# A one-token attention and MLP kernel whose large loads move from SyncE's queue to GpSimd's

## The chip, the cores and the metric

The kernel runs on one core of a Trainium2 chip. The metric is the device time of that core in microseconds (us); lower is better. A profiled execution has a time of its own, and a span, which runs from its first to its last recorded instruction. Engine names are those of the profile: PE is TensorE's matrix multiply, PEld its weight load, DVE is VectorE, ACT is ScalarE, POOL is GpSimd, SP is SyncE. A "q" behind a name (SPq) is that engine's instruction queue, which also issues transfers.

## The reference

One token x of 512 values goes through two branches that a scalar gate mixes.

```python
x = A_x                                             # [1, 1, 512], bf16
g = sigmoid((x * gate_w).sum(-1))                   # one scalar
# attention branch: 32 heads of 128, 4096 cached keys and values a head
q = (x @ wq).reshape(32, 128)                       # wq [512, 4096]
scores = einsum("hd,hkd->hk", q, k_cache) * 128 ** -0.5   # k_cache [32, 4096, 128]
o = einsum("hk,hkd->hd", softmax(scores), v_cache)  # v_cache [32, 4096, 128]
a = o.reshape(4096) @ wo                            # wo [4096, 512]
# MLP branch: 512 -> 1376 -> 512
h = x @ w1 + b1
b = (relu(h) ** 2) @ w2 + b2
out = g * a + (1 - g) * b                           # [1, 1, 512]
```

Nearly all of the data is read once: 32 MiB of keys, 32 MiB of values, 4 MiB each of wq and wo, and 2.7 MiB of MLP weights, 78.3 MB in all. With one token there is little arithmetic for each byte.

## The kernel before

The program is written out by hand for each engine, with semaphores between them. No scheduler or tile pool changes its order.

**Loads.** A head's keys or values make one transfer of 1 MiB: 128 partitions, each with one contiguous row of 8,192 bytes (32 cached positions by 128 values). `Kt` and `Vt` have 8 slots each (`NK`, `NV`). SP issues all large loads, in this order. First come four 1 MiB slices of wq into the tile `W` (L200). Then come the keys of heads 0 to 6 (`LAG` = 7; L206). Then, for each head h, the values of h (L211) and the keys of h+7 (L206). Behind h = 8 go four slices of w1 (L221, 344 KB each), and behind h = 10 the two parts of w2 (L223, L224). When the last use of wq is over (`s_qps` at 8), five pieces of wo follow into the same tile `W` (L227). Last, SP waits for the result and issues the store (L230). From the ninth on, a key load first waits until its slot has been read by DVE (`s_sd`) and by PE (`s_t`), and a value load until PE has read its slot (`s_pv`). SP meets these waits in program order, so whatever is listed behind a waiting load waits too:

```python
def load_k(h):
    if h >= NK:
        eng.wait_ge(s_sd, h - NK + 1)
        eng.wait_ge(s_t, 2 * (h - NK + 1))
    eng.dma_start(Kt[:, h % NK, :], k_h[h, :, :]).then_inc(s_k[h % NK], 16)
```

**Small loads.** ACT issues x, the gate weights and the biases, 1 to 2.5 KB each.

**Constants.** POOL does no transfers. It fills `ident`, `identf`, `onesf`, `negs` and `sel` with memsets (L236 to L240) and turns three of them into patterns (L243, L246). Two semaphores report this: `s_cst` (`onesf` and `negs`) and `s_id`.

**Start of PE.** PE's first matmul (L304) sums the gate's products over partitions with `onesf`. It waits for `s_cst` and for DVE's product (`s_zp`). Its result goes to ACT for an exp (L263, `s_ez`). PE waits for all four slices of wq and for `s_ez` before it makes q (L310), then makes the first rows of q for DVE (`q_rows`, L320), and then waits for all of `s_id`.

**A head.** Half of its scores are made by DVE: 16 multiply-and-sum instructions over 128x128 blocks of `Kt` (`ttr`, L484). The other half goes over PE: 16 transposes (L334), ACT's copy of them (L275) and 16 matmuls (L344). Every four heads the maximum is found and ACT takes the exp. `pv` (L371) multiplies with the values seven steps behind the keys.

**End.** The MLP is put in at steps 24 and 30 (L387, L399). Behind the last head PE regroups the heads and multiplies with wo piece by piece as it lands (`attn_out`, L417). DVE adds (L552), PE transposes, DVE copies (L554), and SP stores.

## Time and profile before

| | |
|---|---|
| median of 3 runs | 202.94 us (202.88 to 203.29) |
| the profiled execution's own time | 203.75 us |
| its span | 202.0 us |
| busy: PE, PEld | 128.6, 115.2 us (64%, 57%) |
| busy: DVE, ACT, POOL | 127.7, 79.4, 2.4 us (63%, 39%, 1%) |
| read from HBM | 78.32 MB, 388 GB/s over the span |
| granted TensorE clock, mean | 0.614 of full speed |

The profile shows the busy time of each engine and of the 16 DMA engines, the chain of work that ended last, the groups of instructions, and what ended each idle stretch. A DMA issue is an instruction of a queue (SPq, ACTq), and is not counted as an engine's busy time; its duration is that of the issue and not of the transfer. "To landing" is from the issue to the last byte. A DMA packet here is one contiguous piece that one of the 16 DMA engines moves.

### The profile page before, as it was taken

How to read it: one execution, taken by the hardware profiler on the slowest of the kernel's cores; microseconds unless marked ns; L12 is line 12 of the kernel's file. 1: busy time of each engine (PE TensorE's matmuls, PEld its weight loads, DVE VectorE, ACT ScalarE, POOL GpSimd, SP SyncE). 2: the span in 40 equal slices, each digit the busy share in tenths (PEclk: the TensorE clock that was granted, in tenths of full speed). 3: DMA queues.
4: the chain of work that ended last, by engine and by line, in shares of the span. 5: the costliest groups of instructions: out<-in, count | busy, mean ns of one | idle time of the engine just before them, and what ended most of it. 6: DMA issues, size and time to landing. Idle time of an engine off the chain costs nothing.

```text
span 202.0 us, 6578 instructions
## 1 busy us (share of the span) xinstructions
PE 128.6 (64%) x2465; PEld 115.2 (57%) x2465; DVE 127.7 (63%) x1134; ACT 79.4 (39%) x147; POOL 2.4 (1%) x12
## 2 busy tenths in 40 slices
PE   0119924956998867528345694569876759864544
PEld 0017824755797667526345674568876759764443
DVE  0200999999999887626645778577877777710000
ACT  2000864566475436305324453435363336320000
POOL 4000000000000000000000000000000000000000
PEclk9999985675555555556655588557555555555555
DMA  5999999999999999999999999999999999999810
GB/s 205 385 395 428 420 420 415 422 417 422 420 419 415 419 413 415 420 426 373 417 425 415 419 417 420 419 422 420 417 417 417 423 417 422 417 419 420 329 66 8
DMA packets 11935, 78.74 MB, mean 390 GB/s; under 512 B 1824, under 2 KB 1920, under 8 KB 2688
## 3 DMA queue, kind: packets, MB, share of 16 engines
q1 hardware_dynamic: 11352, 78.32, 94.1%
q8 instruction: 19, 0.31, 0.6%
q10 hardware_dynamic: 552, 0.01, 0.1%
q14 instruction: 12, 0.10, 0.1%
HBM read 78.32 MB, written 0.00 MB: 388 GB/s over the span
## 4 chain that ended last, share of the span: by engine, by line
DMA 73%; DVE 13%; PE 7%; SPq 4%; issue 1%; ACT 0%; DVEq 0%
DMA Kt<-in_A_k_cache_dram 54%; DMA W<-in_A_wo_dram 13%; DVE Kt L484 12%; DMA W<-in_A_wq_dram 6%; PE KP L334 2%; PE pX L310 2%; PE pQ L320 1%; SPq L223 1%; SPq L206 1%; SPq L227 1%; DVE S L484 1%; SPq L200 1%; SPq L211 1%; PE pX L417 1%; PE pM L358 1%
## 5 line engine op out<-in xcount | busy, mean ns | idle before, releaser
L484 DVE CUSTOM_DVE_ANT_0 Kt<-Kt,qb 128x128 bf16<-128x128 bf16 x512 | 111.3, 286 | 28.5 <-DMA Kt<-in_A_k_cache_dram 28.1
L275 ACT ACTIVATE kT<-KP 128x1024 bf16<-128x1024 bf16 x64 | 61.8, 1021 | 69.3 <-PE KP L334 69.3
L334 PE MATMUL KP<-ident,Kt 128*128 128x128 bf16 x512 | 55.1, 294 | 36.1 <-DMA Kt<-in_A_k_cache_dram 36.0
L334 PEld LDWEIGHTS KP<-ident,Kt 128*128 128x128 bf16 x512 | 47.8, 136 | 38.5 <-DMA Kt<-in_A_k_cache_dram 37.5
L484 DVE DVE_READ_ACCUMULATOR2_ANT S<- 128x1 f32 x512 | 41.6, 81 | 0.0
L344 PE MATMUL pS<-qcol,kT 128*128 128x1 bf16 x512 | 19.3, 167 | 10.6 <-DVE S L490 10.3
L344 PEld LDWEIGHTS pS<-qcol,kT 128*128 128x128 bf16 x512 | 18.8, 107 | 12.2 <-DVE S L490 11.9
L371 PEld LDWEIGHTS pO<-E,Vt 128*128 128x128 bf16 x512 | 15.7, 104 | 1.7 <-issue 1.1
L371 PE MATMUL pO<-E,Vt 128*128 128x1 bf16 x512 | 16.2, 166 | 0.0
L320 PE MATMUL pQ<-W,xb 128*128 128x512 bf16 x32 | 13.8, 581 | 0.0
L267 ACT ACTIVATE qb<-pQ 128x512 bf16<-128x512 f32 x8 | 4.8, 597 | 20.4 <-PE pQ L320 20.3
L371 PE MATMUL pQ<-E,Vt 128*128 128x1 bf16 x256 | 8.0, 165 | 6.0 <-DMA Vt<-in_A_v_cache_dram 6.0
L371 PEld LDWEIGHTS pQ<-E,Vt 128*128 128x128 bf16 x256 | 7.6, 104 | 6.3 <-issue 6.3
L286 ACT ACTIVATE E<-S,nM 128x32 bf16<-128x32 f32 x32 | 9.9, 310 | 0.3
L310 PE MATMUL pX<-xcol,W 128*128 128x1 bf16 x128 | 3.6, 165 | 7.6 <-DMA W<-in_A_wq_dram 7.6
L371 PEld LDWEIGHTS pX<-E,Vt 128*128 128x128 bf16 x256 | 7.6, 101 | 1.0 <-issue 0.8
L310 PEld LDWEIGHTS pX<-xcol,W 128*128 128x128 bf16 x128 | 3.5, 104 | 7.7 <-issue 7.7
L371 PE MATMUL pX<-E,Vt 128*128 128x1 bf16 x256 | 7.8, 164 | 0.0
L472 DVE CAST qcol<-pX 128x32 bf16<-128x32 f32 x1 | 0.2, 192 | 10.4 <-PE pX L310 10.4
L493 DVE TENSOR_REDUCE mp<-S 128x1 f32<-128x32 f32 x32 | 6.0, 186 | 1.1
L417 PE MATMUL pX<-o,W 128*128 128x1 bf16 x128 | 4.1, 166 | 3.8 <-DMA W<-in_A_wo_dram 3.5
L490 DVE COPY S<-pS 128x16 f32<-128x16 f32 x32 | 5.4, 169 | 1.6 <-PE pS L344 1.6
(65 smaller groups left out, 55.2 us busy)
## 6 DMA issues: line engine op xcount, KB each, us to landing
Kt<-in_A_k_cache_dram SPq DMA_DIRECT2D x32, 1024.0 KB, 27.1
Vt<-in_A_v_cache_dram SPq DMA_DIRECT2D x32, 1024.0 KB, 27.3
W<-in_A_wq_dram SPq DMA_DIRECT2D x4, 1024.0 KB, 8.7
W<-in_A_wo_dram SPq DMA_DIRECT2D x3, 1024.0 KB, 22.6
w_sb<-in_B_w_dram SPq DMA_DIRECT2D x4, 344.0 KB, 22.0
w2a<-in_B_w_dram SPq DMA_DIRECT2D x1, 1280.0 KB, 18.1
W<-in_A_wo_dram SPq DMA_DIRECT2D x1, 768.0 KB, 25.6
W<-in_A_wo_dram SPq DMA_DIRECT2D x1, 256.0 KB, 24.1
```

The source lines that it names most:

```text
L267: eng.activation(qb[:, c * 512:(c + 1) * 512], pQ[:, :], ACT.Copy).then_inc(s_qb, 1)
L275: eng.activation(kT[:, h % 2, j * HB * 128:(j + 1) * HB * 128], KP[n % 3][:, :], ACT.Copy).then_inc(s_ev, 1)
L286: eng.activation(E[:, h % NE, :], S[:, h % NS, :], ACT.Exp, bias=nM[:, h:h + 1], scale=SCALE, accum_out=RS[:, h:h + 1]).then_inc(s_e, 1)
L310: mm = eng.matmul(Q[:, h:h + 1], wq_sb[:, t, h * 128:(h + 1) * 128], xcol[:, t:t + 1], start=(t == 0), stop=(t == 3))
L320: mm = eng.matmul(pQ[:, :], xb[:, t, :], wq_sb[:, t, c * 512:(c + 1) * 512], start=(t == 0), stop=(t == 3))
L334: mm = eng.transpose(KP[n % 3][:, y * 128:(y + 1) * 128], Kt[:, h % NK, b * 128:(b + 1) * 128], ident[:, :])
L344: mm = eng.matmul(S2[:, y:y + 1], kT[:, h % 2, y * 128:(y + 1) * 128], qcol[:, h:h + 1], start=True, stop=True)
L371: mm = eng.matmul(O(h, h + 1), Vt[:, h % NV, b * 128:(b + 1) * 128], E[:, h % NE, b:b + 1], start=(b == 0), stop=(b == NB - 1))
L417: mm = eng.matmul(acc[:, j:j + 1], wo_sb[:, t, j * 128:(j + 1) * 128], o2[:, t:t + 1], start=False, stop=(t == 31), skip_group_check=True)
L484: ins = eng.tensor_tensor_reduce(kb, kb, qb[:, h * 128:(h + 1) * 128], 1.0, 0.0, ALU.mult, ALU.add, S[:, h % NS, b:b + 1])
L490: eng.tensor_copy(S[:, h % NS, XB:NB], S2).then_inc(s_cp, 1)
L493: eng.tensor_reduce(mp[:, h:h + 1], S[:, h % NS, :], AX.X, ALU.max).then_inc(s_mp, 1)
```

## The change

The issue of all large loads moves from SP's program to POOL's, in the same order and with the same waits. SP keeps only the store of the result. POOL first issues the four slices of wq and the keys of heads 0 to 6, then makes its constants, and then goes on with the loads. The load of w1 is one transfer of 128 rows of 11,008 bytes instead of four of 128 rows of 2,752 bytes, so PE waits for 16 instead of 64 on `s_w1`. The two parts of w2 report on a semaphore each.

```diff
@@ semaphores
-        s_w2 = sem("s_w2")
+        s_w2 = [sem(f"s_w2{n}") for n in range(2)]
@@ block.sync
         def _(eng):
+            eng.wait_ge(s_f4, 1)
+            eng.dma_start(out[0, 0, :].rearrange("(j p) -> j p", p=128), fin4[:, :]).then_inc(s_out, 16)
+            eng.wait_ge(s_out, 16)
+
+        @block.gpsimd
+        def _(eng):
             for t in range(4):
                 eng.dma_start(wq_sb[:, t, :], wq_v[:, t, :]).then_inc(s_wq[t], 16)
...
             for h in range(LAG):
                 load_k(h)
-            for h in range(NH):
-                load_v(h)
-                if h + LAG < NH:
-                    load_k(h + LAG)
-                if h == 8:
-                    for t in range(4):
-                        eng.dma_start(w1_sb[:, t, :], w1_v[:, t, :]).then_inc(s_w1, 16)
-                if h == 10:
-                    eng.dma_start(w2a[:, :, :], w2_v).then_inc(s_w2, 16)
-                    eng.dma_start(w2b[:, :], B_w2[FG * 128:F, :]).then_inc(s_w2, 16)
-            eng.wait_ge(s_qps, 8)
-            for c in range(NW):
-                eng.dma_start(wo_sb[:, TS[c]:TS[c + 1], :], wo_v[:, TS[c]:TS[c + 1], :])\
-                   .then_inc(s_wo[c], 16)
-            eng.wait_ge(s_f4, 1)
-            eng.dma_start(out[0, 0, :].rearrange("(j p) -> j p", p=128), fin4[:, :]).then_inc(s_out, 16)
-            eng.wait_ge(s_out, 16)
-
-        @block.gpsimd
-        def _(eng):
             eng.memset(ident[:, :], 0.0).then_inc(s_id, 1)
...
             eng.affine_select(out=sel[:, :, :], in_=sel[:, :, :], compare_op=ALU.not_equal, fill=1.0,
                               base=0, pattern=[[1, 4], [-1, 128]], channel_multiplier=4)\
                .then_inc(s_id, 1)
+            for h in range(NH):
+                load_v(h)
+                if h + LAG < NH:
+                    load_k(h + LAG)
+                if h == 8:
+                    eng.dma_start(w1_sb[:, :, :], w1_v).then_inc(s_w1, 16)
+                if h == 10:
+                    eng.dma_start(w2a[:, :, :], w2_v).then_inc(s_w2[0], 16)
+                    eng.dma_start(w2b[:, :], B_w2[FG * 128:F, :]).then_inc(s_w2[1], 16)
+            eng.wait_ge(s_qps, 8)
+            for c in range(NW):
+                eng.dma_start(wo_sb[:, TS[c]:TS[c + 1], :], wo_v[:, TS[c]:TS[c + 1], :])\
+                   .then_inc(s_wo[c], 16)
@@ block.tensor
             def mlp_h():
-                eng.wait_ge(s_w1, 64)
+                eng.wait_ge(s_w1, 16)
...
             def mlp_out():
                 eng.wait_ge(s_hs, 2)
-                eng.wait_ge(s_w2, 32)
+                eng.wait_ge(s_w2[0], 16)
+                eng.wait_ge(s_w2[1], 16)
```

PE, DVE and ACT run the same instructions in the same order as before.

## The prediction

> **What bounds the kernel now.** I read the strip of 40 slices first. It asks whether the transfers ever stop, and from the second slice to the 37th they don't.

> ```profile
> DMA  5999999999999999999999999999999999999810
> GB/s 205 385 395 428 420 420 415 422 417 422 420 419 415 419 413 415 420 426 373 417 425 415 419 417 420 419 422 420 417 417 417 423 417 422 417 419 420 329 66 8
> q1 hardware_dynamic: 11352, 78.32, 94.1%
> DMA 73%; DVE 13%; PE 7%; SPq 4%; issue 1%; ACT 0%; DVEq 0%
> ```

> The DMA engines are at 90% or more nearly throughout, 73% of the chain that ended last is DMA, and one queue moves all 78.32 MB. DVE and PE are about 63% busy and are not the bound. So the end moves if the first byte moves, if the rate moves, or if the queue runs empty. Next I read the table of stretches at its end.

> ```profile
> 20.00:100.00 80.00, 56.34 (x945) 48.77 (x944) 68.75 (x621) 42.24 (x69) 0.00 (x0) 0.60 1.01 416
> 100.00:190.00 90.00, 60.93 (x1239) 57.41 (x1240) 56.32 (x497) 35.41 (x75) 0.00 (x0) 0.56 1.01 418
> 192.00:194.00 2.00, 1.01 (x32) 0.93 (x32) 0.00 (x0) 0.00 (x0) 0.00 (x0) 0.50 0.28 107
> 194.00:196.00 2.00, 1.01 (x32) 0.93 (x32) 0.00 (x0) 0.00 (x0) 0.00 (x0) 0.50 0.08 32
> 196.00:198.00 2.00, 1.01 (x32) 0.93 (x32) 0.00 (x0) 0.00 (x0) 0.00 (x0) 0.50 0.06 25
> ```

> The last two columns are the DMA share and GB/s. The rate is flat at 416 to 418 until 190, which is 26 GB/s for each of 16 engines. At 194 it has fallen to 32 and then 25 GB/s: one engine alone still works. That last engine sets the end, at 198.5 us, and PE's last piece of wo and the store follow in 3.4 us. Instruction fetches (the page's queues "instruction") lie on the same engines, and in the landing records this engine's lag grows in steps of about 1 us, each beside such a fetch. The change touches none of that directly.

> How deep is the queue ahead of the engines? The issue table and SP's timeline tell:

> ```profile
> Kt<-in_A_k_cache_dram SPq DMA_DIRECT2D x32, 1024.0 KB, 27.1
> Vt<-in_A_v_cache_dram SPq DMA_DIRECT2D x32, 1024.0 KB, 27.3
> 0.75 2.10 SPq L200 DMA_DIRECT2D W<-in_A_wq_dram  x4
> 12.35 2.11 SPq L211 DMA_DIRECT2D Vt<-in_A_v_cache_dram  x1
> 24.18 0.33 SPq L206 DMA_DIRECT2D Kt<-in_A_k_cache_dram  x1
> 27.58 0.33 SPq L206 DMA_DIRECT2D Kt<-in_A_k_cache_dram  x1
> 31.31 0.33 SPq L206 DMA_DIRECT2D Kt<-in_A_k_cache_dram  x1
> ```

> A load lands 27 us after its issue, which at 2.48 us for a MiB (the spacing of landings) is some 11 loads ahead. An issue takes 0.33 us where the queue has room, and 2.1 us where it only follows the drain. So SP's own issue time is hidden, and taking it away gains nothing.

> **The change part by part.**

> *76 issues go to POOL* (4 wq, 64 of K and V, w1, two of w2, five of wo; SP had 79 with w1 in four). POOL issues no transfer in this trace, so the price g of one has to be bounded: below by SP's 0.33 us, above by SP's longest key issue, 2.82 us. [...] The wait rows that POOL inherits (SP waited 61.6 us for DVE and PE) stay under the 27 us of queue.

> *First byte.* Nothing hides this one. SP's first issue begins at 0.75 and the first packet starts at 1.95, so 1.2 us. On POOL the issue begins at the same point (its first memset ran at 0.74), and what is added is g minus SP's 0.40 to 0.68 us for an issue of wq: from -0.3 us (g = 0.33) to +2.4 (g = 2.82). I take +0.7, nearer to g = 1 and a little for a slower start. [...]

> *Constants behind eleven loads.* They end at 3.2 us now. Afterwards `onesf` and `negs` come at 0.74 + 11g + 0.6 us.

> ```profile
> 1.16 0.19 POOL L239 MEMSET negs<- 4x128 f32 x1
> 6.45 0.56 PE L304 MATMUL pX<-zp,onesf 128*128 128x1 f32 x2 [6.45 <-DVE zp L459]
> 7.04 0.17 ACT L263 ACTIVATE ez<-pX 128x1 f32<-128x1 f32 x1 [0.83 <-PE pX L304]
> 14.61 3.55 PE L310 MATMUL pX<-xcol,W 128*128 128x1 bf16 x128 [7.60 <-DMA W<-in_A_wq_dram]
> ```

> PE's queue has the gate's sum, then the wait for the exp, then q. From the sum's start to the exp's end it is 0.76 us, and q waits for wq until 14.6. So the constants are hidden if 0.74 + 11g + 0.6 + 0.76 is under 14.6, that is g under 1.13 us. With g = 1 they are. Above it PE, and behind it DVE's first key block at 20.7, start late by 11 (g - 1.13). There is a second cover: the first slot that is waited for comes free at 24.18, and the fourteen loads issued before it keep the engines busy until 38.4 at the earliest (the landing records), which is 14.2 us, less 1.2 to the next first byte. Only g over 1.13 + 13.0 / 11 = 2.3 us reaches the end that way. `s_id` (about 1.8 us behind `negs`) is wanted at 19.9 and has 5 us of room.

> *w1 in one transfer.* A packet of 2,752 B takes 110 ns in the packet records, one of 2,048 B 84, one of 8,192 B 309 and one of 10,240 B 389. That is 9 ns and 27.3 GB/s. 32 packets become 8 of 11,008 B on each engine, so 24 x 9 ns, and three semaphore packets of 9 ns fall away: -0.24 us on the path, sure if the packets are cut as the rows are. PE's wait for it is covered: w1 is read at 139.5, more than 50 us after its landing. The two semaphores of w2 cost one wait, nothing.

> *Rate.* 71 transfers put 568 packets of 8,192 B on each engine. If GpSimd's descriptors cost the same, nothing changes; if they lose or gain one fixed 9 ns a packet, it is 568 x 9 ns = 5.1 us either way. I take no change, because 8,192 bytes in 309 ns is set by bytes for 300 of them.

> *VectorE against POOL.* L484 reads two tiles of SBUF in 128 columns at a time:

> ```profile
> L484 DVE CUSTOM_DVE_ANT_0 Kt<-Kt,qb 128x128 bf16<-128x128 bf16 x512 | 111.3, 286 | 28.5 <-DMA Kt<-in_A_k_cache_dram 28.1
> ```

> The first heads come 3.7 us apart on DVE (the key issues at 24.18, 27.58, 31.31), while their two loads take 4.96. If POOL is held for a whole head's work, 3.7 us, the 27 us of queue cover it. I take nothing. [...]

> *Sum*, against the execution of 203.75 us: +0.7 - 0.24 = +0.46, so 204.2. The median of the runs is 0.81 below that execution; for the median I say 202.94 + 0.46 = 203.4. With the ends of the first byte, and 0.24 off, the case runs from 202.4 to 205.1.

> **The rivals.** (1) *Same rate, later first byte*: the sum, 203.4. For it: flat rate, deep queue.

> (2) *Faster: the fixed part of a packet shrinks.* The place is each of the 568 packets on the last engine. From 0.8 ns a packet (0.46 us) it outweighs the late start; if all 9 ns went, 203.4 - 5.1 = 198.3. For it: the records show 9 ns beside the bytes in every size, and a data packet behind an instruction fetch takes up to 968 ns instead of 309, so the queue's handling does cost time. Against it: nothing shows that another queue handles it better.

> (3) *Slower: descriptors cost transfer time.* One more 9 ns a packet, from descriptors that have to be read or rows cut in two: 203.4 + 5.1 = 208.5. It decides from 0 ns. The strip would show about 408 instead of 418.

> (4) *Slower: issue becomes the bound.* At g = 2.82, 76 x 2.82 + 2.4 for the constants + 0.75, then about 2.5 for the last transfer and 3.4 for the end make a span of 223, so 224. The other road is DVE blocked by POOL: 4.96 - 3.73 = 1.23 us of room a head is used up from 0.61 us for each of two issues, and at 1 us each it is 32 x 0.77 = 25 us. Against both: the idle POOL and the room of 2.48 us.

> That the move does nothing is part of (1), with only w1's 0.24 us left.

> **How the numbers follow.** 0.2% is 0.4 us, about what a measurement of this kernel can tell from no change. (1) gets 0.42: within it 0.05 faster, 0.12 same, 0.25 slower. (2) gets 0.30, nearly all faster. (3) gets 0.18 and (4) 0.10, both slower. So faster 0.34, same 0.13, slower 0.53. The forecast is the likeliest case, 203.4; its own range is 202.4 to 205.1. The range of all reaches down to 198.5 for (2) and up to 208.6 for (3), and leaves out (4) and some edges.

> **What would show it.** Right: DMA at 9 throughout, 415 to 420 GB/s in the middle, first wq landings half a microsecond later, PE's q at about 15, POOL's issues near 1 us, a tail of one engine at 25 GB/s. (2) shows as 425 GB/s or more and packets under 309 ns, (3) as 410 or less, (4) as holes in the DMA strip with PE and DVE waiting on `Kt`, or longer L484. Wrong altogether would be a changed order of landings or a late `onesf` that holds PE beyond 27 us.

## The result, and the profile after

The changed kernel takes 204.42 us (204.31 to 204.61, 4 runs) where the kernel before takes 202.91 (202.83 to 203.29, 4 runs): a ratio of 1.0072, 95% interval 1.0054 to 1.0089. It is slower by 1.5 us. The profiled execution took 204.38 us with a span of 202.6. The experiments below were timed on three chips, each beside 11 to 33 runs of the kernel before, with medians of 203.04 to 203.11; against those the changed kernel is slower by 1.3 to 1.4. Each ratio below is against the runs beside that experiment, and a difference of times from two experiments is uncertain by about 0.2 us.

The execution of the kernel before that the prediction shows took 203.75, which is 0.8 over its median. So the kernel before was profiled once more (the first experiment below), and that execution of 203.11 us is the one to subtract from. Times of a first packet are from the packet records, and those of a landing from the semaphores.

From the page of the changed kernel, the strip of slices, the queue and the chain by engine:

```profile
DMA  4999999999999999999999999999999999999810
GB/s 149 339 429 425 421 416 424 419 414 424 421 416 419 414 417 422 417 431 380 413 421 422 417 416 425 414 421 422 411 422 422 419 413 429 414 416 421 333 73 6
q0 software_dynamic: 10784, 78.32, 93.8%
DMA 37%; issue 26%; DVE 23%; POOL 7%; PE 5%; ACT 0%; POOLq 0%; DVEq 0%
```

The bytes are now on queue q0. The strip is at 9 as before; of the early slices only the first two are lower (149 and 339 for 205 and 385). The chain names less DMA because at several places it is followed back over POOL's waits, though the engines are no emptier. Unlike those of SP and ACT, POOL's issues are counted as busy time, 42.6 us of POOL in all. The table of stretches (DMA share and GB/s are the last two columns):

```profile
20.00:100.00 80.00, 56.29 (x943) 49.23 (x945) 68.73 (x621) 42.43 (x69) 20.01 (x38) 0.61 1.01 417
100.00:190.00 90.00, 61.97 (x1238) 58.56 (x1241) 56.40 (x497) 35.41 (x75) 12.62 (x24) 0.52 1.01 418
192.00:194.00 2.00, 1.01 (x32) 0.93 (x32) 0.00 (x0) 0.00 (x0) 0.00 (x0) 0.50 0.42 167
194.00:196.00 2.00, 1.01 (x32) 0.93 (x32) 0.00 (x0) 0.00 (x0) 0.00 (x0) 0.50 0.10 43
196.00:198.00 2.00, 1.01 (x32) 0.93 (x32) 0.00 (x0) 0.00 (x0) 0.00 (x0) 0.50 0.06 25
```

The rate in the middle is the same, and the tail with one engine at 25 GB/s is there too. The packet records agree: 8,192 B take 309 ns at the 10th and 312 at the 50th percentile in both kernels. The start is in the timeline:

```profile
1.26 2.23 POOL L207 DMA_DIRECT2D W<-in_A_wq_dram  x4 [0.80 <-POOLq L568]
3.49 3.69 POOL L213 DMA_DIRECT2D Kt<-in_A_k_cache_dram  x7
7.60 0.20 POOL L225 MEMSET negs<- 4x128 f32 x1
7.85 0.59 PE L303 MATMUL pX<-zp,onesf 128*128 128x1 f32 x2 [7.85 <-POOL negs L225]
8.47 0.17 ACT L262 ACTIVATE ez<-pX 128x1 f32<-128x1 f32 x1 [3.75 <-PE pX L303]
15.18 3.56 PE L309 MATMUL pX<-xcol,W 128*128 128x1 bf16 x128 [6.74 <-DMA W<-in_A_wq_dram]
```

POOL's first issue shows at 1.26 instead of SP's 0.75, and four issues take 2.23 us. The first packet starts at 2.64 us; it was 1.95 in the execution shown before and 1.77 in the second. The constants come later, and the gate's sum waits for `negs`, but q still waits for wq, until 15.18. Of the costliest groups, the two that the prediction worried about:

```profile
L484 DVE CUSTOM_DVE_ANT_0 Kt<-Kt,qb 128x128 bf16<-128x128 bf16 x512 | 111.3, 287 | 27.5 <-DMA Kt<-in_A_k_cache_dram 26.9
L218 POOL DMA_DIRECT2D Vt<-in_A_v_cache_dram x32 | 17.0, 531 | 95.3 <-PE pO L370 54.9
```

VectorE's instruction takes 287 ns (286 before), and an issue on POOL 531 ns. In the list of issues a load of keys now lands 32.0 us behind its issue and not 27.1: POOL's issues of large loads stay at 0.53 to 0.66 us, where SP's took from 0.33 to 7.24, and POOL runs further ahead.

Then the end. These are rows of the program's closing line, L65: the queue's instruction, its duration in ns (least, median, most), its first and last start. First the kernel before, in its second profiled execution:

```profile
L65 POOLq DRAIN  x1: 1042/1042/1042, 2.2 to 2.2; - x1
L65 SPq DRAIN  x1: 7/7/7, 201.1 to 201.1; - x1
L65 POOLq EVENT_SEMAPHORE  x2: 17/17/17, 201.1 to 201.2; - x2
```

and the changed kernel:

```profile
L65 POOLq DRAIN  x1: 29071/29071/29071, 173.3 to 173.3; - x1
L65 SPq DRAIN  x1: 7/7/7, 201.8 to 201.8; - x1
L65 POOLq EVENT_SEMAPHORE  x2: 17/17/17, 202.4 to 202.5; - x2
```

POOL ends its program with a drain. Before, it ran at 2.2 us where nobody waited for it. Now it stands behind the last issue; its row begins at 173.27, beside the five issues of wo (171.59 to 174.21), and ends at 202.34, 3.15 us behind the last landing (199.19). SP is through with the store at 201.8, so the closing handshake of the engines waits 0.6 us for POOL.

The account between the executions of 203.11 and 204.38 us: the last landing moves from 198.52 to 199.19 (+0.67), and the closing from 0.03 us behind SP's drain to 0.60 behind it (+0.58). Together that is 1.25, which is the whole difference of the two spans (201.32 and 202.57); the times differ by 1.27. Single executions scatter by as much as the first term: in the one of 203.75 us, the last landing was at 199.18. But in the first four experiments, all on the kernel before, it was at 198.41 to 198.62, and in the changed kernel and the two experiments that keep its start (w1 in four transfers, and keys alone on POOL) at 199.10 to 199.23.

### The profile page after: what moved, and what is told of

The parts are those of the page before. It is cut to its first block, busy times and chain, and to the rows that moved or that the text cites. A ratio compares the mean times of both kernels' runs of the same rounds, so it can differ in the third digit from the quotient of the medians.

```text
span 202.6 us, 6569 instructions
## 1 busy us (share of the span) xinstructions
PE 128.8 (64%) x2458; PEld 116.6 (58%) x2465; DVE 127.8 (63%) x1134; ACT 79.5 (39%) x147; POOL 42.6 (21%) x88
## 3 DMA queue, kind: packets, MB, share of 16 engines
q0 software_dynamic: 10784, 78.32, 93.8%
HBM read 78.32 MB, written 0.00 MB: 387 GB/s over the span
## 4 chain that ended last, share of the span: by engine, by line
DMA 37%; issue 26%; DVE 23%; POOL 7%; PE 5%; ACT 0%; POOLq 0%; DVEq 0%
DVE Kt L484 20%; DMA Kt<-in_A_k_cache_dram 19%; DMA W<-in_A_wo_dram 13%; DMA W<-in_A_wq_dram 6%; POOL Vt L218 3%; POOL Kt L213 3%; PE pX L309 2%; DVE S L484 1%; PE KP L333 1%; POOL W L207 1%; POOL W L246 1%; PE pQ L319 1%; DVE S L490 1%; PE pX L417 1%; PE pO L370 0%
## 5 line engine op out<-in xcount | busy, mean ns | idle before, releaser
L484 DVE CUSTOM_DVE_ANT_0 Kt<-Kt,qb 128x128 bf16<-128x128 bf16 x512 | 111.3, 287 | 27.5 <-DMA Kt<-in_A_k_cache_dram 26.9
L333 PE MATMUL KP<-ident,Kt 128*128 128x128 bf16 x512 | 56.3, 298 | 34.0 <-DMA Kt<-in_A_k_cache_dram 34.0
L333 PEld LDWEIGHTS KP<-ident,Kt 128*128 128x128 bf16 x512 | 48.9, 139 | 36.5 <-DMA Kt<-in_A_k_cache_dram 35.4
L484 DVE DVE_READ_ACCUMULATOR2_ANT S<- 128x1 f32 x512 | 42.3, 83 | 0.0
L218 POOL DMA_DIRECT2D Vt<-in_A_v_cache_dram x32 | 17.0, 531 | 95.3 <-PE pO L370 54.9
L213 POOL DMA_DIRECT2D Kt<-in_A_k_cache_dram x32 | 16.9, 531 | 35.0 <-DVE S L484 34.0
L319 PE MATMUL pQ<-W,xb 128*128 128x512 bf16 x25 | 11.6, 603 | 1.7 <-issue 1.7
L505 DVE RECIPROCAL rden<-pM 128x8 f32<-128x8 f32 x4 | 0.8, 202 | 9.6 <-PE pM L376 9.6
## 6 DMA issues: line engine op xcount, KB each, us to landing
Kt<-in_A_k_cache_dram POOLq DMA_DIRECT2D x32, 1024.0 KB, 32.0
Vt<-in_A_v_cache_dram POOLq DMA_DIRECT2D x32, 1024.0 KB, 33.4
W<-in_A_wq_dram POOLq DMA_DIRECT2D x4, 1024.0 KB, 9.0
W<-in_A_wo_dram POOLq DMA_DIRECT2D x3, 1024.0 KB, 22.1
```

The lines of the kernel that those rows point to most:

```text
L218: eng.dma_start(Vt[:, h % NV, :], v_h[h, :, :]).then_inc(s_v[h % NV], 16)
L319: mm = eng.matmul(pQ[:, :], xb[:, t, :], wq_sb[:, t, c * 512:(c + 1) * 512], start=(t == 0), stop=(t == 3))
L333: mm = eng.transpose(KP[n % 3][:, y * 128:(y + 1) * 128], Kt[:, h % NK, b * 128:(b + 1) * 128], ident[:, :])
L484: ins = eng.tensor_tensor_reduce(kb, kb, qb[:, h * 128:(h + 1) * 128], 1.0, 0.0, ALU.mult, ALU.add, S[:, h % NS, b:b + 1])
```

## The experiments

The theory (A) before the first of them: a late first packet, less w1's saving, and a new wait for POOL's drain. The rivals are named in each expectation. A2 is A with the second execution's numbers.

**The kernel before, profiled again.** No edit.

> The kernel before, unchanged, profiled once more. The first profiled execution took 203.75 us, 0.8 us over the median of its timed runs; the changed kernel's took 204.38, at its median. Theory A (the cost is 0.6 us of late first byte, less w1's 0.24, and a new wait of 0.6 us at the end for POOL's drain): an ordinary execution of the kernel before has its last piece of wo landed at about 197.8 us instead of 198.5, its first packet again at 1.95, and a time near 202.9. Rival B (recording itself costs the kernel before 0.8 us and the other nothing): the span is again near 202.0 while the timed runs stay at 202.9.

Measured: 203.07 us, ratio 1.0003 (0.9994 to 1.0012), span 201.3, first packet at 1.77, last landing at 198.52. The first packet is earlier than the 1.95 that was expected. The first shown execution was one of the long ones (the runs of the kernel before reach 203.74); B falls. The piece of wo that PE waits for lands at 197.89 and not 198.54, about as A said.

**w1 in one transfer, on SP.**

```diff
-                    for t in range(4):
-                        eng.dma_start(w1_sb[:, t, :], w1_v[:, t, :]).then_inc(s_w1, 16)
+                    eng.dma_start(w1_sb[:, :, :], w1_v).then_inc(s_w1, 16)
```

> The kernel before with w1 in one transfer, still issued by SP. Theory A: 0.24 us less on each DMA engine, so 202.7 us. Rival (the w1 edit is hidden or costs time): 202.9 or more.

Measured: 202.93, ratio 0.9996 (0.9987 to 1.0005). The expected 0.24 us is 0.12%, inside the interval, and so is nothing at all. Unresolved.

**An extra load of 1 KB on POOL, early or late**, in the kernel before, behind the constants; the late one with the wait, the early one without.

```diff
+            eng.wait_ge(s_wo[3], 16)          # the late one only
+            eng.dma_start(tiny[:, :], A_x[0, 0, :].rearrange("(p j) -> p j", p=128)).then_inc(s_tiny, 16)
```

> The kernel before with one extra load of 1 KB issued by POOL behind its constants at 3.2 us, into a tile that nobody reads. Theory A (POOL's drain at the end waits for the landing of its own loads): the load lands early, the drain ends with it, and the time is that of the kernel before, 202.9 us within 0.2. Rival C (any load issued by POOL makes the drain last until after the others' end): +0.6 us, 203.5.

> The same extra load of 1 KB, but issued by POOL when the fourth piece of wo has landed, near 198.5 us. Theory A: it lands near 200.6, the drain ends 3.2 us behind that as it does in the changed kernel (199.19 to 202.36), so about 203.8, some 2 us beyond the store: 204.8 us in time. Rival C (a fixed cost of having used the queue): 203.5, the same as with the early load. Rival D (the drain waits for descriptors only, not for landings): 202.9.

Measured: early 203.23, ratio 1.0007 (0.9998 to 1.0016); late 202.99, ratio 0.9998 (0.9989 to 1.0006). The late load is a miss of mine. Its rows (the load's issue from the timeline, the drain from L65):

```profile
198.06 0.67 POOL L252 DMA_DIRECT2D tiny<-in_A_x_dram  x1 [194.86 <-DMA W<-in_A_wo_dram]
L65 POOLq DRAIN  x1: 2194/2194/2194, 198.0 to 198.0; - x1
```

The load landed at 200.15 and the drain ended at 200.23. So the drain lasted until the landing (D falls), but it ended 0.08 us behind it, and not 3.15. The early load shows the same: it landed at 9.51 and the drain ended at 9.58. Neither a fixed cost of using the queue (C) nor a fixed time behind the landing is right. What differs is the number of loads that POOL issued, 1 against 76. The next runs put numbers on that: by loads issued, or by loads still in flight.

**The first eleven loads on SP**, in the changed kernel.

```diff
@@ block.sync
+            for t in range(4):
+                eng.dma_start(wq_sb[:, t, :], wq_v[:, t, :]).then_inc(s_wq[t], 16)
+            for h in range(LAG):
+                eng.dma_start(Kt[:, h, :], k_h[h, :, :]).then_inc(s_kf[h], 16)
@@ block.gpsimd
-            for t in range(4):
-                eng.dma_start(wq_sb[:, t, :], wq_v[:, t, :]).then_inc(s_wq[t], 16)
...
-            for h in range(LAG):
-                load_k(h)
+            eng.wait_ge(s_kf[3], 16)          # behind the constants
```

> The changed kernel, but SP issues the four slices of wq and the keys of heads 0 to 6 again (the first keys with semaphores of their own), POOL makes its constants at the start and goes on with the other 65 loads when the keys of head 3 have landed. Theory A2 (two costs: a first packet 0.87 us later, and POOL's drain, which ends 3.17 us behind the last landing and so 0.6 us behind the rest): the first packet is at about 1.8 instead of 2.64, the last piece of wo lands near 198.4 instead of 199.19, the drain's end moves with it, and the time is 203.6 us, 0.8 under the changed kernel. Rival K (the late start is hidden and the whole cost is at the end): 204.4. On the drain: if it costs 42 ns for each load that POOL has issued (76 gave 3.17 us), 65 give 2.7 us behind the last landing; if it goes by the loads in flight when it begins, it is 3.2 us again.

Measured: 203.08, ratio 0.9999 (0.9990 to 1.0008): level with the kernel before, and under the changed kernel by 1.3 (by the times) to 1.5 (by the ratios).

```profile
L65 POOLq DRAIN  x1: 28620/28620/28620, 172.9 to 172.9; - x1
L65 SPq DRAIN  x1: 7/7/7, 201.4 to 201.4; - x1
```

The rows are from the longest of its 12 runs, 203.57 us. The first packet is at 1.91, the last landing at 198.81, and the drain ends at 201.51, 2.70 behind it: the 42 ns for each of 65 loads. The expected 203.6 counted the earlier packet and forgot the shorter drain: 204.42 - 0.87 - 11 x 0.042 = 203.1. Here POOL ends only 0.1 us behind SP. K falls: with the start hidden, a drain that is 0.46 us shorter would have left 204.0. And 65 loads on POOL's queue cost nothing else beyond the interval, 0.2 us either way.

**The constants ahead of all loads.** In POOL's program the block from the memset of `ident` to the last `affine_select` goes ahead of the loads of wq.

> The changed kernel with POOL's constants made ahead of all loads instead of behind the first eleven. Theory A2 (the end follows the first packet one for one): the constants take 2.4 us (0.74 to 3.17 in the kernel before), the first packet comes at about 5.1 instead of 2.64, and the time is 204.4 + 2.4 = 206.8 us. Rival K (the queue has room, the start is hidden): 204.4.

Measured: 205.14, ratio 1.0098 (1.0085 to 1.0111). The sign is as expected and the size is not: +0.7 over the changed kernel (0.5 by the ratios) instead of +2.4. The first packet is at 4.55, 1.91 later, and the last landing at 199.96, only 0.77 later. The stretches of 5 us (last column GB/s), first the changed kernel:

```profile
0.00:5.00 5.00, 0.00 (x0) 0.00 (x0) 0.52 (x5) 1.49 (x2) 3.95 (x11) 1.00 0.48 145
5.00:10.00 5.00, 0.59 (x2) 0.50 (x2) 0.97 (x7) 0.17 (x1) 4.76 (x14) 1.00 0.91 338
10.00:15.00 5.00, 0.00 (x0) 0.00 (x0) 0.00 (x0) 0.00 (x0) 1.20 (x3) 1.00 1.01 426
```

then with the constants first:

```profile
0.00:5.00 5.00, 0.56 (x2) 0.50 (x2) 0.52 (x5) 1.55 (x3) 4.22 (x16) 1.00 0.17 26
5.00:10.00 5.00, 0.00 (x0) 0.00 (x0) 0.88 (x7) 0.00 (x0) 5.00 (x10) 1.00 0.95 393
10.00:15.00 5.00, 0.00 (x0) 0.00 (x0) 0.00 (x0) 0.00 (x0) 0.58 (x2) 1.00 1.02 431
```

The bytes of 15 us differ by 5 x (145 + 338 + 426 - 26 - 393 - 431) = 295 KB, which at 418 GB/s is 0.71 us. So the end does follow the bytes, but the first packet is a poor measure of them: the changed kernel starts in a slow phase (338 GB/s) that a later start partly avoids. What makes that phase slow, no run isolates.

**wo on SP**, in the changed kernel.

```diff
@@ block.sync
+            eng.wait_ge(s_qps, 8)
+            eng.wait_ge(s_v[(NH - 2) % NV], 16 * ((NH - 2) // NV + 1))
+            for c in range(NW):
+                eng.dma_start(wo_sb[:, TS[c]:TS[c + 1], :], wo_v[:, TS[c]:TS[c + 1], :])\
+                   .then_inc(s_wo[c], 16)
```

> The changed kernel, but SP issues the five pieces of wo, when the values of head 30 have landed, so that POOL's last load is the values of head 31. Theory A2: the last landing stays near 199.2, POOL's drain ends some 3 us behind the landing of head 31's values (189.3), long before the store, and the 0.6 us at the end are gone: 203.8 us. Rival K2 (the drain is not what ends last): 204.4. On the drain's length: 42 ns for each of 71 loads gives 3.0 us behind the landing; by the loads in flight at its start (7 instead of 12), 1.8.

The same, with the first eleven loads on SP too:

> Both edits together: SP issues the first eleven loads and the five pieces of wo, POOL the 60 between. Theory A2: both costs are gone and what is left is w1 in one transfer, 202.8 to 203.0 us, level with the kernel before. If POOL's queue also moves bytes more slowly or holds VectorE back, it stays above 203.4.

Measured: 204.89, ratio 1.0096 (1.0083 to 1.0109), and 204.20, ratio 1.0047 (1.0035 to 1.0060). Both miss, and the fault is in the experiment. From the page of the first, and its drain from L65:

```profile
DMA  5899999999999999999999999999999999972990
GB/s 163 319 430 423 423 417 422 420 417 420 419 420 409 422 423 415 420 422 384 419 420 417 420 419 419 420 420 420 412 422 420 422 419 420 415 309 56 391 408 16
L65 POOLq DRAIN  x1: 21156/21156/21156, 171.2 to 171.2; - x1
```

My wait for head 30's values lets wo go only at 187, when the rate had fallen: 56 GB/s in the 37th slice. The late engine was to hide that, but in the next two slices wo came at 391 and 408 GB/s, and the third piece landed 3.86 us behind the second (2.47 in the changed kernel), so the last landing came at 200.73. The drain's length is read all the same: it ended at 192.36, 2.95 behind head 31's values for 71 loads, and 2.50 for the 60 of the second kernel. By the loads in flight 1.8 was expected; that falls.

**Values, MLP weights and wo on SP, keys on POOL**, to take the drain off the end and keep the late start, without that wait.

```diff
@@ block.sync
+            eng.wait_ge(s_k[3], 16)
+            for h in range(NH):
+                load_v(h)
...
+            eng.wait_ge(s_qps, 8)
+            for c in range(NW):
+                eng.dma_start(wo_sb[:, TS[c]:TS[c + 1], :], wo_v[:, TS[c]:TS[c + 1], :])\
+                   .then_inc(s_wo[c], 16)
@@ block.gpsimd
-            for h in range(NH):
-                load_v(h)
...
+            for h in range(LAG, NH):
+                load_k(h)
```

> The changed kernel, but POOL issues only wq and the 32 loads of keys; SP issues the values (from the landing of the keys of head 3 on), the MLP weights and wo, in the same order among themselves. The first packet stays late, as in the changed kernel, and POOL's last load lands long before the end. Theory A2: the 0.6 us at the end are gone (the drain is 36 loads x 42 ns behind the last keys, hidden) and the 0.67 us at the last landing stay: 203.8 us. Rival K2 (what ends last is not the drain): 204.4. If only the drain costs and the late start is hidden: 203.1.

Measured: 203.83, ratio 1.0043 (1.0031 to 1.0055), with the first packet at 2.64 and the last landing at 199.10.

```profile
L65 POOLq DRAIN  x1: 34606/34606/34606, 132.8 to 132.8; - x1
L65 SPq DRAIN  x1: 7/7/7, 201.7 to 201.7; - x1
L65 POOLq EVENT_SEMAPHORE  x2: 17/17/17, 201.7 to 201.8; - x2
```

The drain ended at 167.42, off the path, and the closing follows SP at once. This is the drain by itself: 204.42 to 203.83, 0.6 us by the times and by the ratios, and in the traces the closing moves by 0.58. What stays, 0.7 over the kernel before (0.9 by the ratio), is there with a first packet at 2.64 and gone in the experiment with the first eleven loads on SP; so it is put down to the late start. K2 falls.

**w1 in four transfers again**, in the changed kernel (the diff of the second experiment, turned round, on POOL).

> The changed kernel with w1 in four transfers again, issued by POOL. Theory A2: 24 packets and three semaphore packets of 9 ns come back on each DMA engine (0.24 us on the last landing), and POOL's drain lengthens by three loads of 42 ns (0.13 us): 204.4 + 0.37 = 204.8 us. Rival (the w1 edit is hidden): 204.4.

Measured: 204.60, ratio 1.0076 (1.0062 to 1.0089). The drain ended 3.27 us behind the last landing, 0.12 longer for three loads more, as expected. The last landing moved by only 0.04 (199.23), where 0.24 was expected. The packet records have a reason: on POOL's queue the four transfers went out as 256 packets of 5,504 B, two rows each, and not as the 512 of 2,752 B that SP's queue had. So only 8 packets and three semaphore packets come back on each engine, by my estimate 0.1 us at the 9 ns of the kernel before. w1's edit is worth a little on POOL, and mostly because it saves three loads.

**The loads of b1 later**, in the kernel before with w1 in one transfer; ACT issues them at step 12, and DVE waits for them ahead of the MLP.

```diff
-            eng.dma_start(b1a[:, :], col(B_b1[0:FG * 128])).then_inc(s_b, 16)
-            eng.dma_start(b1b[:, :], B_b1[FG * 128:F].rearrange("(p j) -> p j", j=1)).then_inc(s_b, 16)
...
+                if i == 12:
+                    eng.dma_start(b1a[:, :], col(B_b1[0:FG * 128])).then_inc(s_b1, 16)
+                    eng.dma_start(b1b[:, :], B_b1[FG * 128:F].rearrange("(p j) -> p j", j=1)).then_inc(s_b1, 16)
```

> The kernel before with w1 in one transfer and with the two loads of b1 (224 rows of 20 and of 2 bytes) issued by ACT some 60 us later, out of the first 12 us. With the constants ahead of the loads the first packet came 1.91 us later but the last landing only 0.77, because the first slices of wq, which meet the small loads, then took 2.5 us each instead of 3.5 at the worst. Theory S (rows of a few bytes hold up the large loads wherever they meet them): the first slices get quicker, the later ones lose the same, and the time stays at 202.9. Rival T (only the start suffers): 0.5 to 1 us less, 202.2.

Measured: 202.82, ratio 0.9988 (0.9979 to 0.9997). It is the one version that is faster than both kernels beyond its interval, by 0.12%. The stretch from 5 to 10 us, first of the kernel before (second execution), then of this one:

```profile
5.00:10.00 5.00, 0.56 (x2) 0.50 (x2) 0.88 (x7) 0.38 (x2) 0.00 (x0) 1.00 1.01 409
```

```profile
5.00:10.00 5.00, 0.56 (x2) 0.50 (x2) 0.90 (x7) 0.38 (x2) 0.00 (x0) 1.00 1.03 423
```

The start is quicker (423 for 409, and 428 for 395 in the next 5 us). Over the first 15 us that is 5.27 MB, and the eight other executions with SP's loads first have 4.83 to 5.03. So the rows of b1 are part of what slows it. But 202.82 is nearer to S (202.9) than to T (202.2): most is lost again later. Against the kernel with only w1 changed, 202.93, the gain isn't resolved.

**The last MiB of wo in transfers of 8 rows**, in the kernel before with w1 in one transfer, to find the late engine.

```diff
+            for c in range(NW - 2, NW):
+                for r in range(16):
+                    eng.dma_start(wo_sb[8 * r:8 * r + 8, TS[c]:TS[c + 1], :],
+                                  wo_v[8 * r:8 * r + 8, TS[c]:TS[c + 1], :]).then_inc(s_wo[c], 16)
```

> The kernel before with w1 in one transfer, and with the last two pieces of wo (1 MiB) issued as 32 transfers of 8 partitions each instead of two of 128. The last landing is set by one DMA engine that is 4.4 us behind the next. Theory L: a transfer of 8 rows goes to eight of the sixteen engines only. If the late engine is among the other eight, it has 2.5 us less to do, the tail shortens to the engines that took the extra work, and the time is about 201; if it is among the eight, it has 2.5 us more, and the time is 205.5. Rival (rows spread over all sixteen as before): 203.0.

Measured: 209.99, ratio 1.0340 (1.0326 to 1.0354), beyond every number expected. SP needed 22.33 us for the 32 issues, until 194, and the last landing came at 205.5, 11.5 us behind the end of the issue; of its last landing signals one came each 0.2 us. So transfers of 8 rows were slow in themselves here, and the run doesn't say which engine is late. What slowed them is not shown.

## Why the prediction was right, and where it was short

The measured 204.42 lies inside the range of 202.4 to 205.1, and the bound and the cost of a late start were read rightly. But the upper part of that range stood there for an issue of up to 2.82 us, which took 0.53. That a cost of 0.6 us that the sum didn't have still fell inside it is luck.

**The bound: right.** 417 and 418 GB/s in the middle and packets of 309 to 312 ns, as before. Rivals (2) and (3), a packet cheaper or dearer by 9 ns, fall.

**The price of an issue, g: too high, and harmless.** 1 us was taken, and no run shows it: it was an estimate. POOL's issues took 0.53 us (0.66 the first); the bounds 0.33 and 2.82 held it. It hid behind the 2.48 us of a load, and so did the constants: `negs` at 7.8 us, the exp at 8.6, and q waiting for wq until 15.18. Rival (4) falls on both roads; POOL's issues took 0.53 us each while VectorE worked, and L484 took 287 ns (286 before). (Its time is 225 and not 224, since a span of 223 is 1.8 us short of the time.)

**The first packet: right in size, wrong in make-up.** +0.7 was taken, an estimate from g = 1, which no run shows, and a little for a slower start; it is +0.69 against the execution that the sum was made on, +0.87 against the second. But the first issue is only 0.26 us longer than SP's (0.66 for 0.40), where g = 1 would have made it 0.6. Another 0.51 us lie ahead of it: "on POOL the issue begins at the same point" is wrong, since POOL's first issue shows at 1.26 us and SP's at 0.75, though a memset as POOL's first instruction starts at 0.75 (the experiment with the constants first).

**VectorE against POOL: right.** Nothing was taken for it, and nothing shows: beside each other an issue on POOL took 0.53 us and L484 287 ns (286 before).

**w1: mis-sized.** -0.24 was called sure. On SP, where the packets are cut as the rows are, it measured -0.04% with an interval of 0.09% on either side. On POOL, where four transfers have two rows of w1 to a packet, it was 0.04 us at the last landing. Between the first packet's +0.87 and the last landing's +0.67 some 0.2 us were regained; how much of that is w1's stays open.

**What was missing: POOL's drain.** The prediction followed the move to the first issue and to the constants, and not to the end of POOL's queue. The row was there in the profile of before: a drain of 1,044 ns at 2.2 us, at the end of POOL's program and ahead of the closing handshake. Moving 76 loads onto that queue put the drain behind them, and it ended 3.15 us behind their last landing, which is 41 ns for each. The 0.6 us of that on the path are the largest part of what the forecast of +0.46 lacks to the measured +1.5 on the medians (1.3 to 1.4 against the later runs of the kernel before); w1's 0.24, which didn't show, is the next. Without the drain on the path the kernel takes the 203.83 of the experiment above, 0.7 over the kernel before.

## What to carry to other kernels

Here the transfer stream kept the DMA engines at 90% or more, and with the loads on POOL the rate in the middle stayed at 417 to 418 GB/s. Where a profile looks like that, don't change the engine that issues for its issue time; ask what the move does to the first packet (0.87 us later here) and to the end of each queue. Count the closing wait of a queue as one of the instructions that move (0.58 us here): look up the program's last line in the profile for both queues, and see which one ends last. If POOL must issue loads, let another queue issue the first and the last of them (203.08 and 203.83 us here, for 204.42), but issue the last ones early enough that the rate holds (56 GB/s in a slice and 204.89 us with wo at 187). Each of the two was shown to help by itself here; the kernel that had both also had the late wo (204.20).
